# A list scheduler for TensorE in four quarters, with a new table of places, in a kernel of attention and two gated MLPs

## The chip, the cores and the metric

The kernel runs on one core of one Trainium2 chip. The metric is device time in microseconds of one execution. Three runs of the kernel before took 618.84, 619.43 and 620.29 us; their median is 619.43 us.

## What is computed

Four batches of 448 positions and 12 heads of 64 columns go through an attention with normed queries and keys, then through a gated MLP, then through a second one. Inputs are float32 values; the weights come to the kernel in 64-bit words. Cut to what matters:

```python
q_n, k_n = rmsnorm(q, g_q), rmsnorm(k, g_k)            # (4, 12, 448, 64)
attn = softmax(scale * q_n @ k_n.T); x = attn @ v      # -> (4, 448, 768)
h = relu(x @ w_in)                                     # 768 -> 1024
x = (h * sigmoid(conv3(h))) @ w_out                    # 1024 -> 768
y = (sigmoid(causal_conv5(x)) * (x @ w_val)) @ w2_out  # 768 -> 768
```

## The kernel before

Nothing is issued where it is written. The code calls a recorder, `Plan`, in place of the engines. `at(t, fn)` gives each step of the work (an event) a nominal time t; the events are sorted by it and run once, and each engine call in them becomes an operation with its data dependences, its possible engines ("ways") and its event's time. `Plan.order()` then simulates the chip and puts all operations in one order, and `Plan.emit` issues them in that order. All instructions of the profile therefore carry the line of `emit`, L545, and are told apart by their tiles.

The order comes from a list scheduler. An operation's urgency (`first`) is made of its event's nominal time, the length of work behind it (`tail`) and its event's entry in the table `OFFSETS`, which moves the operations of that event earlier or later by that many us. `forward` keeps a clock for each engine; again and again it takes the engine that can start something first, and of the operations that can start by then the most urgent one. For TensorE an operation of another shape than the one before (up to 64 rows, up to 64 columns, or neither) has `SWITCH` added to its urgency, and 0.1 us to its cost. `backward` finds the latest times, `MIX` blends these into the urgencies, and the best of `PASSES` passes is kept. Operations of one engine stay in the order found; between engines semaphores hold them to their data.

In the old clock TensorE is one engine that does one matmul after the other. A matmul whose output starts at a partition above 0, or that has 64 rows of input in the upper half, is costed at 0.022 us, because it runs beside the one before it.

The work: a unit is 128 query positions of two heads (or the 64 left over, of two pairs of heads). Its scores are matmuls of 64 rows, one head in the upper half of the rows and one in the lower, three float16 products each (high and low parts) or, for the groups in `FLAT`, one in float32. VectorE multiplies by the root of q's norm and finds the row maxima (`smax`), ScalarE takes the exponential, a high and a low part are made (`phi`, `plo`), a DMA or TensorE transposes, and `av` multiplies by the values. There are 21 units to a batch, 84 in all. The two MLPs of a batch run beside the attention of the next one; their matmuls have 128 rows and 448 or 384 columns. Batch 3's MLPs have nothing beside them.

Norms: `sum_q` and `sum_k` square and sum; `FOLD_Q0` to `FOLD_Q3` say how many times the squares are first folded in half on GpSimd. `rroots` takes the inverse root by three steps: with `ROOT_POOL` of the batch 0, three VectorE instructions each, with 1, four that may go to VectorE or GpSimd. `LEAVE_IN` of a batch says whether the gated tile leaves PSUM for SBUF (its low part can then be made on GpSimd), `X_SBUF` the same for the attention's result.

Times of the parts are in constants: `S_TQ` the nominal time at which the first group's q is turned, `W_IN` to `W_2` of the weights, `L_...` and `PC_...` what is added to an operation's cost on one of its ways when an engine is chosen.

Of the kernel before, what the change touches and what calls it, by code (L numbers as in the profile page):

```python
# [176 lines left out]
class Plan:  # L177
# [12 lines left out]
    AHEAD = 39.506  # L190
    URGENT = 0.644
    TICK = 10.24 / 3
    ENTRY = 3060.0

    SWITCH = 2.538

    PASSES = 4
    MIX = 0.913

    KEEP = 0.002  # L200

    SLACK_T = 1.769
    SLACK_L = 0.399
    CUSH = 0.0
# [344 lines left out]
def kernel(  # L549
# [540 lines left out]
    def prep(b, r, t0, tq, dq, tk_, dk, ahead):  # L1090
# [91 lines left out]
        def gain_k(i):  # L1182
            if flat:
                return
# [735 lines left out]
```

## Time and profile before

| | |
|---|---|
| span of the profiled execution | 618.4 us |
| the profiled execution's own time | 620.15 us |
| median of three runs | 619.43 us |
| TensorE matmuls busy | 594.4 us, 4747 instructions |
| VectorE busy | 491.2 us, 1124 instructions |
| ScalarE busy | 412.0 us, 797 instructions |
| GpSimd busy | 276.7 us, 330 instructions |

PE is TensorE's matmul, PEld its weight loads, DVE VectorE, ACT ScalarE, POOL GpSimd, SP the queue that issues most DMAs. A busy time is the union of an engine's instructions; matmuls are pipelined, so the time from one start to the next is shorter than the length of one. Some matmul records can be missing from a trace, so counts of matmuls in a row may be low. A wait is the idle time of an engine just before an instruction, put down to the last thing that released it.

### The profile page before, as it was taken

The numbers are of one execution on the slowest core, as the hardware profiler recorded it, in microseconds if no ns is written. First come the engines' busy times: TensorE is split into PE (matmuls) and PEld (weight loads), VectorE is DVE, ScalarE is ACT, GpSimd is POOL, SyncE is SP. The second block draws the span as 40 slices with busy tenths as digits, with TensorE's granted clock in tenths as the row PEclk, the third lists the DMA queues.
The fourth block names the chain that finished last, engine by engine and source line by source line (L and its number), as shares of the span: only waits on it lengthen the run. The fifth ranks groups of instructions, "written<-read, shape, count | busy, mean of one in ns | idle before, by whom it ended". The sixth has DMA issues, their size and how long they took to land.

```text
span 618.4 us, 12831 instructions
## 1 busy us (share of the span) xinstructions
PE 594.4 (96%) x4747; PEld 346.3 (56%) x4747; DVE 491.2 (79%) x1124; ACT 412.0 (67%) x797; POOL 276.7 (45%) x330
## 2 busy tenths in 40 slices
PE   5999999998999999999999999999999999999997
PEld 2666776555666555455555556455555656555554
DVE  6899999999999987898789785699898543567820
ACT  4887988889869886896567645778766543352221
POOL 2243644456755879587365751733564210140000
PEclk9999999999999999999999999999999999999999
DMA  7866649686839498975898579865564658000002
GB/s 205 195 153 166 164 124 242 149 206 135 165 103 225 99 181 159 215 185 130 176 158 144 112 161 192 155 118 100 92 127 95 117 120 136 14 1 1 1 13 77
DMA packets 230805, 82.10 MB, mean 133 GB/s; under 512 B 216864, under 2 KB 226646, under 8 KB 230742
## 3 DMA queue, kind: packets, MB, share of 16 engines
q1 hardware_dynamic: 229541, 79.71, 60.5%
q10 hardware_dynamic: 1200, 1.57, 1.0%
q8 instruction: 37, 0.61, 0.4%
q14 instruction: 27, 0.21, 0.1%
HBM read 38.59 MB, written 5.51 MB: 71 GB/s over the span
## 4 chain that ended last, share of the span: by engine, by line
PE 52%; DVE 24%; ACT 9%; DMA 6%; POOL 4%; issue 4%; SPq 1%; ACTq 0%; DVEq 0%; POOLq 0%
PE ps L545 52%; DVE ps L545 6%; DVE act L545 5%; DVE scr L545 4%; DVE w L545 4%; ACT p L545 3%; DMA pt<-p 2%; DVE half L545 2%; DMA act<-in_moe_w_out_dram 1%; ACT act L545 1%; SPq L545 1%; DVE ssq L545 1%; POOL tq L545 1%; DVE p L545 1%; POOL tk L545 1%
## 5 line engine op out<-in xcount | busy, mean ns | idle before, releaser
L545 PE MATMUL ps<-act,wo 128*128 128x448 f16 x576 | 125.4, 353 | 1.5 <-ACT ka L545 0.8
L545 DVE TENSOR_SCALAR_CACHE_REDUCE ps<-ps,root 128x448 f32<-128x448 f32 x168 | 109.3, 686 | 20.2 <-PE ps L545 19.8
L545 PE MATMUL ps<-act,wi 128*128 128x448 f16 x576 | 118.4, 353 | 1.3 <-DVE scr L545 0.7
L545 ACT ACTIVATE p<-ps,mx 128x448 f32<-128x448 f32 x154 | 91.4, 632 | 19.2 <-POOL mx L545 7.8
L545 PE MATMUL ps<-vv,pt 128*128 128x65 f16 (+5 forms) x1440 | 103.4, 206 | 0.0
L545 PE MATMUL ps<-w,act 128*128 128x384 f16 (+1 forms) x576 | 93.3, 327 | 0.9 <-ACT w L545 0.9
L545 POOL TENSOR_TENSOR p<-p,p 128x896 f16<-128x896 f32 x32 | 61.4, 1921 | 68.4 <-ACT p L545 59.3
L545 PE MATMUL ps<-act,wv 128*128 128x448 f16 x432 | 91.9, 353 | 0.0
L545 PE MATMUL ps<-ka,qa 64*128 64x448 f16 (+3 forms) x512 | 86.5, 415 | 2.5 <-ACT ka L545 1.3
L545 PEld LDWEIGHTS <-wi 128*128 128x128 f16 x576 | 53.7, 98 | 53.9 <-issue 9.2
L545 PEld LDWEIGHTS <-wo 128*128 128x128 f16 x576 | 55.1, 100 | 48.7 <-issue 8.1
L545 PEld LDWEIGHTS <-pt 128*128 128x128 f16 (+1 forms) x1344 | 64.0, 101 | 26.7 <-issue 7.8
L545 ACT ACTIVATE act<-ps 128x448 f16<-128x448 f32 (+3 forms) x80 | 42.4, 534 | 45.6 <-PE ps L545 25.2
L545 PEld LDWEIGHTS <-act 128*128 128x128 f16 (+1 forms) x576 | 48.6, 101 | 31.1 <-issue 5.3
L545 DVE SCALAR_TENSOR_TENSOR act<-ps,cw,act 128x446 f32<-128x446 f32 (+2 forms) x96 | 63.7, 674 | 0.7
L545 PEld LDWEIGHTS <-wv 128*128 128x128 f16 x432 | 40.9, 98 | 37.1 <-issue 3.0
L545 ACT ACTIVATE p<-p 128x896 f16<-128x896 f32 x56 | 53.2, 951 | 3.0 <-DMA pt<-p 2.5
L545 DVE SCALAR_TENSOR_TENSOR w<-w 128x768 uint32<-128x768 uint32 (+1 forms) x56 | 46.6, 832 | 0.4 <-POOL w L545 0.4
L545 DVE SCALAR_TENSOR_TENSOR scr<-ps,cw,scr 128x447 f32<-128x447 f32 x64 | 41.6, 673 | 0.8 <-ACT scr L545 0.7
L545 DVE TENSOR_TENSOR p<-p,p 128x896 f16<-128x896 f32 x24 | 28.5, 1188 | 12.7 <-ACT p L545 12.0
L545 ACT ACTIVATE osb<-ps 128x384 f32<-128x384 f32 x28 | 13.6, 489 | 32.7 <-PE ps L545 28.4
L545 DVE SCALAR_TENSOR_TENSOR act<-ps,act 128x448 f16<-128x448 f32 x48 | 29.7, 618 | 7.0 <-ACT act L545 7.0
(134 smaller groups left out, 938.9 us busy)
## 6 DMA issues: line engine op xcount, KB each, us to landing
w<-in_moe_w_in_dram SPq DMA_DIRECT2D x8, 768.0 KB, 5.9
w<-in_moe_w_out_dram SPq DMA_DIRECT2D x8, 768.0 KB, 4.5
kin<-in_k_dram SPq DMA_DIRECT2D x24, 224.0 KB, 3.5
qin<-in_q_dram SPq DMA_DIRECT2D x36, 128.0 KB, 3.2
act<-in_moe_w_out_dram SPq DMA_DIRECT2D x12, 384.0 KB, 4.1
w<-in_moe_w_val_dram SPq DMA_DIRECT2D x12, 384.0 KB, 3.3
out_dram<-osb SPq DMA_DIRECT2D x19, 192.0 KB, 2.6
vst<-in_v_dram SPq DMA_DIRECT2D x16, 224.0 KB, 3.6
```

Source lines behind the costliest of these rows:

```text
L545: getattr(getattr(nc, e), method)(*a, **k)
```

## The change

Three things change.

First, the clock in `forward`. TensorE has four quarters, `parts`: rows below or above 64 by columns below or above 64. A matmul occupies the quarters that it uses until its end; the next one starts when its own quarters are free, and no sooner than `ISSUE` (0.022 us) after the one before. One that follows another TensorE operation by data is ready `ISSUE` after that one's start. Second halves now have their full cost.

Second, the table `OFFSETS` is another: 820 entries in place of 1411, and about forty constants have other values.

Third, new options in the program, all off in the new constants (`K_PE`: keys turned by TensorE with float16 parts; `HALVES`: the transposes of a unit in two DMAs), and six options set otherwise: `FOLD_Q1` 0 to 1, `LEAVE_3` 1 to 0, `XSB_3` 1 to 0, `ROOTP_0` 0 to 1, `ROOTP_2` and `ROOTP_3` 1 to 0. TensorE's matmuls are the same ones as before.

```diff
 OFFSETS = {
...
-    ENTRY = 3060.0
-
-    SWITCH = 2.538
+    ENTRY = 3060.0
+    ISSUE = 0.022
+
+    SWITCH = 2.173
...
-    MIX = 0.913
-
-    KEEP = 0.002
-
-    SLACK_T = 1.769
-    SLACK_L = 0.399
+    MIX = 0.915
+
+    KEEP = 0.053
+
+    SLACK_T = 1.906
+    SLACK_L = 0.332
...
-            if self.region(out)[0] or (a[1].shape[0] == 64 and self.region(a[2])[0]):
-                return 0.022, f * n * a[1].shape[0] / (256 if self.region(out)[0] else 128), 0
-            return 0.0024 + f * max(n, 128 if wide else 64) / 2400, f * n * a[1].shape[0] / 128, 0
+            half, cols = a[1].shape[0] <= 64, a[0].shape[0] <= 64
+            rows = (2 if self.region(a[2])[0] else 1) if half else 3
+            part = (rows << 2 if self.region(out)[0] else rows) if cols else rows | rows << 2
+            columns = f * n * a[1].shape[0] / (256 if self.region(out)[0] else 128)
+            return 0.0024 + f * max(n, 128 if wide else 64) / 2400, columns, part
...
+        def taken(part):
+            return max(x for j, x in enumerate(parts) if part >> j & 1)
...
+        parts = [0.0] * 4
 
         def begin(i, e):
             t = max(free[e], hold[e], ready[i])
+            if e == "tensor":
+                t = max(t, taken(ops[i][0][e][0][2]))
...
+                before = max(t, *parts)
+                for j in range(4):
+                    if data >> j & 1:
+                        parts[j] = t + busy
...
-            free[e] = t + busy
+            free[e] = t + (self.ISSUE if e == "tensor" else busy)
+            if e == "tensor":
+                busy = max(0.0, t + busy - before)
...
-                hop = 0.0 if method.startswith("dma") or e == "tensor" == next(iter(ops[u][0])) else self.HOP[e] + self.CUSH
-                ready[u] = max(ready[u], end + hop)
+                hop = 0.0 if method.startswith("dma") else self.HOP[e] + self.CUSH
+                inside = e == "tensor" == next(iter(ops[u][0]))
+                ready[u] = max(ready[u], t + self.ISSUE if inside else end + hop)
...
-    S_TQ = 2.948
+    S_TQ = 4.204
...
-    FOLD_Q1 = 0
+    FOLD_Q1 = 1
...
-    LEAVE_3 = 1
+    LEAVE_3 = 0
...
-    XSB_3 = 1
-    ROOTP_0 = 0
+    XSB_3 = 0
+    ROOTP_0 = 1
     ROOTP_1 = 0
-    ROOTP_2 = 1
-    ROOTP_3 = 1
+    ROOTP_2 = 0
+    ROOTP_3 = 0
```

## Rows read from the trace of the kernel before

**Rows 1.** The page, engines: busy us, share of the span, instructions.

```profile
PE 594.4 (96%) x4747; PEld 346.3 (56%) x4747; DVE 491.2 (79%) x1124; ACT 412.0 (67%) x797; POOL 276.7 (45%) x330
```

**Rows 2.** Table by stretches: length; busy us of PE, PEld, DVE, ACT, POOL; clock; DMA.

```profile
0.00:15.00 15.00, 7.85 (x26) 4.20 (x26) 9.73 (x47) 6.69 (x11) 4.01 (x28) 1.00 0.80 207
15.00:55.00 40.00, 38.26 (x268) 27.31 (x269) 35.61 (x98) 34.95 (x72) 14.60 (x10) 1.00 0.75 181
55.00:95.00 40.00, 38.20 (x327) 27.77 (x326) 38.51 (x105) 33.90 (x67) 19.22 (x24) 1.00 0.52 149
95.00:138.00 43.00, 41.55 (x325) 23.80 (x326) 41.94 (x92) 36.04 (x67) 19.89 (x15) 1.00 0.80 193
138.00:191.00 53.00, 50.76 (x334) 31.10 (x332) 51.65 (x110) 44.61 (x90) 33.03 (x35) 1.00 0.63 143
191.00:400.00 209.00, 203.87 (x1800) 113.14 (x1801) 173.29 (x381) 150.25 (x292) 135.19 (x174) 1.00 0.82 163
400.00:525.00 125.00, 123.96 (x1163) 70.93 (x1161) 93.28 (x218) 78.19 (x151) 41.55 (x38) 1.00 0.61 113
525.00:600.00 75.00, 75.00 (x404) 39.24 (x402) 47.16 (x81) 24.44 (x46) 9.20 (x9) 1.00 0.02 4
600.00:618.40 18.40, 14.98 (x109) 8.78 (x107) 0.00 (x0) 2.94 (x6) 0.00 (x0) 1.00 0.22 74
```

**Rows 3.** Chain of waits: start us, us, what; 138 to 192 us, and the end.

```profile
184.08 1.35 DVE ps L545 x4
...
523.96 91.04 PE ps L545 x532
```

**Rows 4.** TensorE's waits from 15 to 600: total us, times, longest us.

```profile
PE ps L545 <- ACT p L545: 2.7, 6, 0.9
PE ps L545 <- DMA pt<-p: 2.7, 3, 1.0
PE ps L545 <- ACT act L545: 1.6, 4, 0.6
...
PE ps L545 <- issue: 0.2, 1, 0.2
```

**Rows 5.** Timeline of TensorE at 524 and 296: start us, us, what, count.

```profile
524.69 10.57 PE L545 MATMUL ps<-act,wi 128*128 128x448 f16 x55
...
296.16 0.32 PE L545 MATMUL ps<-w,act 128*128 128x384 f16 x1
296.42 1.31 PE L545 MATMUL ps<-ka,qa 64*128 64x448 f16 x12
297.66 0.24 PE L545 MATMUL ps<-vv,pt 128*128 128x64 f16 x2
```

**Rows 6.** Instruction groups (first 15 to 191, then whole span): busy us, mean ns, idle before.

```profile
L545 DVE TENSOR_SCALAR_CACHE_REDUCE ps<-ps,root 128x448 f32<-128x448 f32 x67 | 43.6, 685 | 4.0 <-PE ps L545 4.0
...
L545 DVE TENSOR_REDUCE ssq<-tq 128x14 f32<-128x896 f32 x6 | 6.4, 1062 | 0.0
...
L545 POOL TENSOR_TENSOR act<-scr,act 128x448 f16<-128x448 f32 x16 | 16.7, 1048 | 18.2 <-ACT act L545 14.9 <-DVE act L545 3.1
...
L545 DVE TENSOR_TENSOR act<-ps,act 128x448 f16<-128x448 f32 x16 | 9.7, 613 | 0.4 <-ACT act L545 0.4
```

**Rows 7.** Timeline of TensorE, float32 scores early and later.

```profile
11.31 3.20 PE L545 MATMUL ps<-ka,qa 64*128 64x448 f32 x8 [0.72 <-ACT ka L545]
14.44 0.51 PE L545 MATMUL ps<-ident,act 112*128 112x112 f32 x3
...
43.62 1.77 PE L545 MATMUL ps<-ka,qa 64*128 64x448 f32 x8 [0.61 <-ACT ka L545]
45.33 0.24 PE L545 MATMUL ps<-ident,act 24*128 24x24 f32 x1
```

**Rows 8.** The root's scratch tile: VectorE 15 to 62; durations ns min/median/max on GpSimd.

```profile
15.00:62.00 47.00, 5.32 (x20) 1.00 0.69 171
...
L545 POOL TENSOR_SCALAR half<-half x11: 222/223/1092, 216.4 to 456.5; 128x30 f32<-128x30 f32 x11
```

More of the change, by code (lines that the diff above doesn't have):

```diff
@@ L539, in forward @@
                     enter(u)
-        return result, max(free.values()), ends
+        return result, max(*free.values(), *parts), ends
     def emit(self, nc):
@@ L698 @@
     EARLY_W = 20
-    S_TQ = 2.948
-    S_DQ = 0.06
+    S_TQ = 4.204
+    S_DQ = 0.005
     S_K0 = 1.209
     S_K1 = 10.195
-    S_DK = 0.153
+    S_DK = 0.207
     S_LQ = 5.919
@@ L709 @@
     DT_2 = 6.044
-    DT_3 = 5.846
+    DT_3 = 5.855
     LAG = 2
@@ L713 @@
     C_GATE = 1.818
-    C_MUL = 2.115
+    C_MUL = 1.881
     C_HI = 2.538
-    C_LO = 3.349
+    C_LO = 3.529
     V_HI = 0.217
@@ L726 @@
     M_1 = -6.504
-    M_2 = -4.505
+    M_2 = -5.284
     M_3 = 4.463
-    D_IN = 2.169
+    D_IN = 2.515
     APART = 2.77
@@ L754 @@
     QD_ = 1.286
-    W_IN = -79.472
+    W_IN = -73.121
     W_IN_STEP = 0.252
@@ L758 @@
     W_OUT_STEP = 1.141
-    W_VAL = 21.2
+    W_VAL = 21.552
     W_VAL_STEP = 0.724
@@ L771 @@
     OUT_3 = 4
+    KPE0_1 = 0
+    KPE0_2 = 0
+    KPE1_0 = 0
+    KPE1_1 = 0
+    KPE1_2 = 0
+    KPE2_0 = 0
+    KPE2_1 = 0
+    KPE2_2 = 0
+    KPE3_0 = 0
+    KPE3_1 = 0
+    KPE3_2 = 0
+    HALF_0 = 0
+    HALF_1 = 0
+    HALF_2 = 0
+    HALF_3 = 0
     WIDE_0 = 1
@@ L789 @@
     L_ROOT = 0.045
-    L_QHI = -0.43
+    L_QHI = 0.252
     L_QLO = -0.306
@@ L793 @@
     L_NORM = 3.224
-    L_KHI = 1.704
-    L_KLO = 0.731
-    L_GLO = 1.042
+    L_KHI = 1.991
+    L_KLO = 0.724
+    L_GLO = 2.877
     L_MUL = 0.171
     L_MXA = 0.2
-    L_RS = 0.452
+    L_RS = 0.419
     MUL = 0.0
@@ L819 @@
     PC_M = 9.047
-    PC_X = 8.979
-    PC_G = 9.0
+    PC_X = 9.243
+    PC_G = 9.307
     PC_F = 8.843
-    PC_S = 0.3
+    PC_S = 0.265
     L_WF = 1.0
@@ L828 @@
     L_VHI = 1.568
-    L_VLO = 1.414
+    L_VLO = 1.035
     L_PHI = 2.172
-    L_PT = 4.537
+    L_PT = 4.191
     L_XHI = -0.121
-    L_GHI = 0.283
+    L_GHI = 0.44
     WIDE = [(0, r) for r, w in enumerate((WIDE_0, WIDE_1, WIDE_2)) if w]
@@ L842 @@
     FK = (FOLD_K0, FOLD_K1, FOLD_K2, FOLD_K3)
+    HALVES = (HALF_0, HALF_1, HALF_2, HALF_3)
     X_SBUF = (0, XSB_1, XSB_2, XSB_3)
@@ L845 @@
     FLAT = [(0, 0)] + [x for x, f in (((0, 1), FLAT0_1), ((0, 2), FLAT0_2), ((1, 0), FLAT1_0), ((1, 1), FLAT1_1)) if f]
+    K_PE = [((0, 1), KPE0_1), ((0, 2), KPE0_2), ((1, 0), KPE1_0), ((1, 1), KPE1_1), ((1, 2), KPE1_2), ((2, 0), KPE2_0), ((2, 1), KPE2_1), ((2, 2), KPE2_2), ((3, 0), KPE3_0), ((3, 1), KPE3_1), ((3, 2), KPE3_2)]
+    K_PE = [x for x, f in K_PE if f]
     events = []
@@ L1099, in prep @@
         flat = (b, r) in FLAT
+        k_pe = flat or (b, r) in K_PE
         g = b * NPR // 2 + r
@@ L1182, in gain_k @@
         def gain_k(i):
-            if flat:
+            if k_pe:
                 return
@@ L1191, in norm_k @@
             holds["tk", i if b == 0 or NTK == 2 else 0] = b, j
-            if flat:
+            if k_pe:
                 by = rr[:KR, cols(i)].rearrange("p (h c) -> p h c", h=2).unsqueeze(3).to_broadcast([KR, 2, KC, D])
@@ L1202, in low_k @@
             assert holds["kin", i] == holds["tk", i if b == 0 or NTK == 2 else 0] == (b, j)
-            if not flat:
+            if not k_pe:
                 sub(lean(L_KLO, S_LK), lo, x, hi)
@@ L1209, in turn_k @@
             holds["ka", (b * NPR + j) % NKA] = b, j
-            if flat:
+            if k_pe:
                 x = o.rearrange("p a c d -> p (a c d)").bitcast(F32).rearrange("p (c d) -> p c d", c=KC)
@@ L1214, in turn_k @@
                     nc.tensor.transpose(ps[:, c * KR : (c + 1) * KR], x[:, c], ident[:KR, :KR])
+                if not flat:
+                    to = ka[(b * NPR + j) % NKA]
+                    times(L_PT, to[:, 0], ps[:, 0:S], gcol)
+                    fma(to[:, 1], ps[:, 0:S], gcol, to[:, 0], ALU.subtract)
+                    return
                 times(L_PT, ka[(b * NPR + j) % NKA].rearrange("p a t -> p (a t)").bitcast(F32), ps[:, 0:S], gcol)
@@ L1359, in ptr @@
         u.t = pt[u.n % u.bufs]
+        if HALVES[u.b]:
+            for a in range(2):
+                turned(out=u.t[:, a * NB : (a + 1) * NB], in_=u.o[:, a].rearrange("p h t -> p (h t)"))
+            return
         turned(out=u.t, in_=u.o.rearrange("p a h t -> p (a h t)"))
```

233 rows, old and new, of the table OFFSETS are left out of this document.

## The prediction

> **What bounds the kernel now.** I read the engines' totals first. TensorE's matmuls are busy 594.4 of 618.4 us, 96%; VectorE has 79% and ScalarE 67% [rows 1]. So about 24 us of span hold no matmul, and everything else lies under matmuls. The profiled execution took 620.15 us, 1.75 more than its span; the sum below is made against it. It stands 0.7 above the 619.43 of the runs shown and inside their spread.
>
> Then the table by stretches [rows 2] says where the 24 us are: 7.15 in the first 15 us (loads and the first norms), 1.74 from 15 to 55, 1.80 to 95, 1.45 to 138, 2.24 to 191, 5.13 to 400, 1.04 to 525, none from 525 to 600, and 3.42 at the end, where the last result is evacuated and stored. The reader is to see a second thing in it: from 55 to 191 VectorE has 38.51 of 40, 41.94 of 43 and 51.65 of 53 us, as full as TensorE. The chain of waits agrees: in that part it goes from one VectorE piece to the next, and from 523.96 it is one run of 532 matmuls, 91.04 us long [rows 3]. What is won before 523 us therefore shifts the rest as a block and reaches the end whole.
>
> Third, what TensorE waited for between 15 and 600 us [rows 4]: ten releasers, of which the first three and the last stand in the rows, 12.6 us together, none above 2.7. Some 9.7 of them are on pieces of ScalarE, VectorE or GpSimd, at most 0.9 us at a time, 2.7 on the DMA that transposes the probabilities. These waits are short and spread; they are the kind that an order of instructions makes or unmakes. The order is what this change rewrites.
>
> Last, the matmuls themselves. In the last stretch 55 full-array matmuls of 448 columns take 10.57 us, with 0.35 for the last one's own length 0.189 each [rows 5]. Twelve matmuls of 64 rows, two score units in one block, take from 296.42 to 297.66, 1.24 us: six times 0.189 plus about 0.1. So the two halves of a pair run at once, and the second costs nothing. The matmul of 384 columns before them (0.162 by its columns) has the next one 0.26 behind it: a block of 64-row work costs some 0.1 us at its entry and 0.1 at its exit. I counted 93 blocks of half-array work in the timeline, the first at 11.31 us [rows 5, 7]: 93 x 0.2 = 18.6 us that no idle column shows.
>
> **The change, part by part.**
>
> *The clock in quarters.* The old clock charges 22 ns for every second half; the chip charges nothing. That overcharge is, in the plan: 48 float16 score units x 3 pairs x 22 ns = 3.2 us, 8 remainder score units x 3 x 66 = 1.6, their 8 value products x 21 x 22 = 3.7, four remainder output tiles x 18 x 22 = 1.6, float32 units about 1.4: 11.5 us over the program. On the chip TensorE reaches its next operand earlier than the plan thinks, and that is where short waits come from. The new clock leaves at most one 22 ns issue per block, 2 us. It removes no matmul. What it can remove is bounded by the 12.6 us of waits [rows 4] below and by none above; a new order can also make as many new ones. I take a third, 4.2 us: the waits on other engines' pieces (9.7) are the ones that better times touch, the DMA's 2.7 and the order's own trade-offs stay. What is late next is VectorE, which between 55 and 191 has only 3.9 us left over its three windows [rows 2].
>
> *Blocks of half-array work.* With quarters, a pair's successor in the same quarter may start 22 ns before any full-array matmul, so a ready pair goes first whatever its urgency, and units merge more often; the extra for a change of shape falls from 2.538 to 2.173, which pulls the other way. I take 5 blocks fewer, 5 x 0.2 = 1.0 us; bounds 15 fewer (-3.0) and 7 more (+1.4).
>
> The Trainium skill, in "TensorEngine Tiling (Array Packing)", section Key Properties, says that a change of tiling mode drains the engine while different tiles run at the same time. By its rule the unit merged away is the gain and not the second half; the 0.1 us at entry and exit [rows 5] agree with it.
>
> *Work moved off VectorE early.* The root of batch 0 may go to GpSimd step by step: two groups that aren't first, of eleven VectorE instructions each, nine of them in the three steps. From 15 to 62 us VectorE spends 5.32 us on 20 of these 22 [rows 8], 0.27 each, so the steps are 18 x 0.27 = 4.8 us. The squares of q in batch 1 are folded once on GpSimd, so three sums of 896 elements, 1.06 us each, become half as long (-1.6) against three additions on GpSimd. GpSimd is 36 to 62% busy there [rows 2]. On TensorE this is worth nothing beyond the third above, since it idles only 1.74 us from 15 to 55. Bounds: -2 and, if GpSimd's slower root is late, +1.
>
> *Work moved back onto VectorE late.* Batch 3 keeps its gated tile and its x in PSUM: eight subtractions leave GpSimd (1.05 us) for VectorE (0.61) [rows 6], and six on tiles of 384 instead of 448 columns likewise, 8 x 0.61 + 6 x 0.53 = 8.1 us of VectorE. The eight belong to the last stage, where VectorE has 47 of 75 us [rows 2]; the six come with batch 3's values, mostly before 525, where it has 93 of 125. The roots of batches 2 and 3 lose their choice of GpSimd and three instructions in twelve. Cover: TensorE from 400 on waits 1.04 us in all, so nothing is gained and nothing lost. If the cover goes, a PSUM bank is held 0.6 us longer; bound +1.
>
> *The start.* The first group's q is turned 1.26 us later by its nominal time. The first score pairs take 0.78 us each, four from 11.31 to 14.44; four later ones, from 43.62 to 45.33, take 1.71 us with the 0.2 of their block, 0.38 each [rows 7]: at the start TensorE runs at half rate, the lower (1.2 GHz) of its two levels, though the granted clock of that window reads 1.00. Where the change to the higher one falls is a matter of phase. I take 0. Bounds: -1.6, half of those 3.13 us, and +1.6.
>
> *The end.* Evacuation and store, 3.42 us, unchanged: 0.
>
> Sum: -4.2 - 1.0 = -5.2. Span 618.4 - 5.2 = 613.2, the execution 1.75 more, 614.95, and the runs' median 0.7 below the profiled one, 614.3. I say 614.5.
>
> **The rivals.**
>
> *A, no change.* The waits don't come from the clock's error but from what no clock knows: when a semaphore arrives, how long a transpose lands. For it: ten releasers, none dominant [rows 4]. Against: most are compute pieces, and these have steady lengths, as the row maxima at 685 ns in the mean of 67 [rows 6]. Then as many waits return, at 619.4, give or take 1.2.
>
> *B, slower.* The rule that a ready pair goes before a full-array matmul displaces the matmuls that feed VectorE. A block of one unit is 0.57 + 0.2 = 0.77 us, and where VectorE has no queue it stands idle for it. From 15 to 191 us there are 67 row maxima, 33 units [rows 6], and from 55 us on VectorE has 4% left or less [rows 2]. If every third block hits, that is 11 x 0.77 = 8.5 us later, less some 4 of the forecast's gain: +4.5, 624. It decides from seven hits on (5.4 us, the whole gain). For it: the full VectorE. Against: VectorE's own waits for TensorE in that time are 4.0 us before row maxima [rows 6], so its queue is mostly filled.
>
> *C, GpSimd blocked.* A root step on GpSimd has a median of 0.22 us and a maximum of 1.09 [rows 8]. If all twelve steps of a group were that long, 13.1 us against VectorE's 9 x 0.27 = 2.4, 10.7 late; the nominal lead of k is 3.236 units of 2.39 us, 7.7, so 3.0 late for each of two groups, +6.0 on the forecast: 620.5. The Trainium skill, "SBUF — State Buffer", section Who interferes with whom, gives the reason: a VectorE instruction with two SBUF inputs and a GpSimd one that reads SBUF exclude each other for a whole instruction. The maximum agrees with it, the median says that it is rare.
>
> **How the numbers follow.** Changes under 0.2% (1.24 us) can't be told from none here. Forecast 0.56, its own range 608.5 to 618; A 0.15; B 0.24; C 0.05. The low end is two thirds of the waits and ten blocks (-8.4 - 2.0, 609), a little below for the start; the high end is B, 623.5. Faster: the forecast and a quarter of A, 0.59. Same: the rest of A's middle, half of C and the edges of the others, 0.15. Slower: B, the rest of C and A's upper edge, 0.26.
>
> **What would show it.** TensorE's waits from 15 to 600 at 8 to 9 us instead of 12.6, its busy time down by about 1 through fewer blocks, VectorE below 95% between 55 and 95. The last stretch of pure matmuls keeps its 91 us and starts about 5 earlier. Wrong: waits of 12 or more (A), VectorE idle behind TensorE between 55 and 191 (B), TensorE or ScalarE waiting for the root (C), or TensorE's busy time up by 2 or more, which means more blocks.

## The result, and the profile after

The changed kernel takes 614.02 us (median of 20 runs, 612.15 to 620.60); the kernel before took 620.84 in 20 runs beside it (618.84 to 624.19). The ratio is 0.9901, with a 95% interval of 0.9883 to 0.9919: about 1% faster. The profiled execution took 614.43 us with a span of 612.6, so 5.8 less span than before.

The runs of the changed kernel differ by TensorE's granted clock, which has to be known to read what follows: the five runs with a clock of 1.000 over the whole program have a median of 612.94 us, the run with the lowest, 0.988, took 620.60. Of the kernel before most runs have 0.999 or 1.000, 48 of the 66 that stand beside the experiments below.

The engines' totals of the changed kernel (busy us, share of the span, instructions), the answer to [rows 1]:

```profile
PE 588.7 (96%) x4747; PEld 344.4 (56%) x4747; DVE 483.8 (79%) x1145; ACT 413.8 (68%) x796; POOL 270.8 (44%) x301
```

The same 4747 matmuls keep TensorE busy for 5.7 us less than in [rows 1]: that is as much as the span lost. Idle time hardly changed, 23.9 us against 24.0. The table by stretches, with the columns of [rows 2], says where it lies:

```profile
0.00:15.00 15.00, 7.72 (x25) 4.33 (x26) 9.70 (x47) 6.70 (x11) 4.30 (x28) 1.00 0.81 209
15.00:55.00 40.00, 37.69 (x274) 28.32 (x274) 36.69 (x91) 33.23 (x66) 15.25 (x21) 0.96 0.70 160
55.00:95.00 40.00, 36.68 (x340) 28.62 (x338) 37.16 (x100) 36.65 (x71) 22.95 (x38) 1.00 0.57 158
95.00:138.00 43.00, 42.38 (x349) 24.57 (x348) 38.23 (x80) 40.20 (x77) 30.81 (x25) 1.00 0.85 195
138.00:191.00 53.00, 51.06 (x348) 31.45 (x346) 52.26 (x124) 44.29 (x88) 30.27 (x36) 1.00 0.66 153
191.00:400.00 209.00, 203.99 (x1796) 112.15 (x1796) 168.88 (x404) 148.70 (x289) 127.71 (x126) 1.00 0.82 164
400.00:525.00 125.00, 124.99 (x1151) 69.89 (x1150) 93.65 (x224) 74.40 (x142) 39.49 (x32) 1.00 0.62 110
525.00:600.00 75.00, 75.00 (x408) 39.76 (x407) 47.22 (x82) 27.66 (x53) 0.00 (x0) 1.00 0.03 9
600.00:612.60 12.60, 9.17 (x74) 5.30 (x71) 0.00 (x0) 1.97 (x4) 0.00 (x0) 1.00 0.24 79
```

From 15 to 95 us TensorE is idle for 5.63 us (2.31 and 3.32), where it was 3.54 before; from 95 to 525 it is idle for less than before in each window, and from 400 to 600 it never stops. Waits were moved to an earlier place, not removed; the DMA that transposes the probabilities is nearly gone from them (0.4 after 2.7), and others took its place. From 15 to 55 the granted clock is 0.96, a number that [rows 2] doesn't have anywhere.

TensorE's waits from 15 to 595 us (total us, times, longest us), the answer to [rows 4]. There are eight releasers, and together they make 12.8 us; ten made 12.6 before:

```profile
PE ps L500 <- DVE scr L500: 3.7, 5, 1.8
PE ps L500 <- ACT p L500: 2.8, 4, 1.3
PE ps L500 <- ACT pt L500: 2.8, 4, 1.2
...
PE ps L500 <- DMA pt<-p: 0.4, 1, 0.4
```

The longest single wait is 1.8 us, against 1.0 before [rows 4]. The chain of waits from 408.90 us to 609.18 is TensorE alone; its second half:

```profile
508.12 101.07 PE ps L500 x661
```

**Where the 5.7 us of matmul time were.** The next table counts only the matmuls of the scores (the tile `ka`): window, its length, busy us and records of PE, clock. First the kernel before, then the changed one:

```profile
0.00:55.00 55.00, 16.79 (x47) 1.00 0.76 188
55.00:138.00 83.00, 21.79 (x98) 1.00 0.67 171
...
sum 525.00, PE 86.55; mean PE 17.31
```

```profile
0.00:55.00 55.00, 15.08 (x46) 0.97 0.73 174
55.00:138.00 83.00, 17.35 (x100) 1.00 0.72 177
...
191.00:400.00 209.00, 26.24 (x210) 1.00 0.82 164
400.00:525.00 125.00, 12.88 (x120) 1.00 0.62 110
sum 525.00, PE 81.13; mean PE 16.23
```

The scores became 5.42 us shorter, and they are the same scores. The timeline of TensorE shows how. In the kernel before, one head of a float32 score unit, then other work, then a head alone again (start us, us, what, count; the time of a block is read from its start to the start of the row behind it):

```profile
28.81 1.02 PE L545 MATMUL ps<-ka,qa 64*128 64x448 f32 x2
29.76 1.09 PE L545 MATMUL ps<-ident,p 128*128 128x128 f32 x8
30.78 1.02 PE L545 MATMUL ps<-ka,qa 64*128 64x448 f32 x2
31.73 0.55 PE L545 MATMUL ps<-ident,p 128*128 128x128 f32 x3
```

In the changed kernel both heads stand in one block:

```profile
31.85 1.02 PE L500 MATMUL ps<-ka,qa 64*128 64x448 f32 x4
32.80 0.55 PE L500 MATMUL ps<-ident,act 128*128 128x128 f32 x2
```

One head alone takes 0.95 us (28.81 to 29.76, 30.78 to 31.73), both together take 0.95 (31.85 to 32.80). In float16 it is the same: a lone head (kernel before) and a pair (changed kernel) take 0.67 each:

```profile
273.40 0.74 PE L545 MATMUL ps<-ka,qa 64*128 64x448 f16 x3
274.07 0.30 PE L545 MATMUL ps<-vv,pt 128*128 128x64 f16 x4
```

```profile
272.79 0.74 PE L500 MATMUL ps<-ka,qa 64*128 64x448 f16 x6
273.46 0.34 PE L500 MATMUL ps<-vm,pt 128*128 128x130 f16 x3
```

So the second half of a pair costs nothing only where it runs beside the first. The timeline of before has 12 lone float32 heads, that of after 5; a pair is 0.95 together and 1.90 apart, so this is (12 - 5) / 2 x 0.95 = 3.3 us. In float16 it is 8 blocks of a lone head against 7, 0.3 us. The rest isn't divided here. Part of it is the entry and exit of blocks of half-array work: there are 15 changes of shape fewer, 173 after 188, which is 7 or 8 blocks. At the prediction's 0.2 us for a block that is an estimate of 1.5 us, and some of it is in the 3.3 already, since a pair that is rejoined is also a block less.

**Which part of the change joined them.** The old clock charged 0.022 us for a second half wherever it stood, so nothing kept the two heads together. That this is the reason is argued, not shown. In the order as issued, 116 of the 168 pairs of score products have another TensorE operation between their heads in the kernel before, and 32 in the changed one; but that count misleads. Of the 116, 94 have only other score products of the same block there, and such a block costs no more: six float16 products issued as first, first, second, second, first, second head take 0.68 us (329.36 to 330.04, kernel before), issued as first, second, second, first, second, first 0.67 (the block at 272.79). Pairs that other work splits are 22 in the kernel before and 23 in the changed one. What fell is the dear kind: 6 of the 22 are float32, and 3 of the 23 (one of their six lone heads stands in a block with a pair, so that the timeline shows five).

Nor are two heads in one block always as cheap as a pair. Of these two blocks of the changed kernel, of four float32 heads each, the first is issued as first, second, second, first head and takes 1.70 us (97.14 to 98.84), the other as first, first, second, second, and takes 2.69 (100.37 to 103.06):

```profile
97.14 1.77 PE L500 MATMUL ps<-ka,qa 64*128 64x448 f32 x8
...
100.37 2.76 PE L500 MATMUL ps<-ka,qa 64*128 64x448 f32 x8
```

In e2 the second one is issued as first, second, first, second and takes 2.22 us (104.97 to 107.19). So the order is a part of it; what the rest waits for is not shown.

**The clock that is lost early.** The timeline of the changed kernel at 41 us, with the waits in brackets:

```profile
41.07 1.77 PE L500 MATMUL ps<-ka,qa 64*128 64x448 f32 x8
43.99 0.24 PE L500 MATMUL ps<-ident,act 24*128 24x24 f32 x1 [1.15 <-DVE scr L500]
...
45.32 1.30 PE L500 MATMUL ps<-ident,p 128*128 128x128 f32 x7 [0.83 <-ACT p L500]
46.55 2.28 PE L500 MATMUL ps<-ka,qa 64*128 64x448 f32 x4
48.76 2.02 PE L500 MATMUL ps<-ident,act 128*128 128x128 f32 x11
50.61 0.40 PE L500 MATMUL ps<-vm,pt 128*128 128x130 f32 x2
```

After two waits of 1.15 and 0.83 us, a group of four score matmuls takes 2.21 us (46.55 to 48.76), where the same four take 1.37 in e12 below (46.63 to 48.00). The window from 46 to 50 has a granted clock of 0.59, so most of it is at 1.2 GHz, the lower of the two levels:

```profile
46.00:50.00 4.00, 4.00 (x14) 2.49 (x15) 3.89 (x13) 3.33 (x7) 1.47 (x2) 0.59 0.12 23
```

Those four microseconds count as busy time; part of the gain is given back there without an idle column showing it. The clock of 0.997 over the profiled span says how much: 0.003 x 612.6 = 1.8 us.

### The profile page after: what moved, and what is told of

It is laid out like the page before. It is cut to its first block, busy times and chain, and to the rows that moved or that the text cites. A ratio compares the mean times of both kernels' runs of the same rounds, so it can differ in the third digit from the quotient of the medians.

```text
span 612.6 us, 12783 instructions
## 1 busy us (share of the span) xinstructions
PE 588.7 (96%) x4747; PEld 344.4 (56%) x4747; DVE 483.8 (79%) x1145; ACT 413.8 (68%) x796; POOL 270.8 (44%) x301
## 4 chain that ended last, share of the span: by engine, by line
PE 70%; DVE 14%; ACT 5%; DMA 4%; issue 3%; POOL 2%; SPq 1%; DVEq 0%; ACTq 0%; POOLq 0%
PE ps L500 70%; DVE act L500 3%; DVE w L500 3%; DVE ps L500 3%; DMA act<-in_moe_w_out_dram 2%; DVE scr L500 2%; ACT act L500 1%; DVE half L500 1%; DVE ssq L500 1%; ACT p L500 1%; DMA w<-in_moe_w_out_dram 1%; DMA ka<-tk 1%; SPq L500 1%; DVE root L500 1%; ACT w L500 1%
## 5 line engine op out<-in xcount | busy, mean ns | idle before, releaser
L500 PE MATMUL ps<-act,wo 128*128 128x448 f16 x576 | 123.1, 353 | 1.1 <-DVE act L500 1.1
L500 POOL TENSOR_TENSOR p<-p,p 128x896 f16<-128x896 f32 x40 | 76.5, 1915 | 65.5 <-ACT p L500 51.7
L500 PE MATMUL ps<-act,wv 128*128 128x448 f16 x432 | 90.3, 353 | 0.3 <-DVE act L500 0.3
L500 PE MATMUL ps<-w,act 128*128 128x384 f16 (+1 forms) x576 | 88.5, 326 | 0.4 <-ACT osb L500 0.4
L500 PE MATMUL ps<-ka,qa 64*128 64x448 f16 (+3 forms) x512 | 81.1, 418 | 0.8 <-ACT ka L500 0.7
L500 PE MATMUL ps<-vv,pt 128*128 128x65 f16 (+5 forms) x1440 | 80.0, 205 | 0.2 <-ACT pt L500 0.2
L500 ACT ACTIVATE act<-ps 128x448 f16<-128x448 f32 (+4 forms) x89 | 46.8, 532 | 42.1 <-DVE ps L500 21.9
L500 PEld LDWEIGHTS <-act 128*128 128x128 f16 (+1 forms) x576 | 48.5, 101 | 33.4 <-issue 5.0
L500 DVE SCALAR_TENSOR_TENSOR act<-ps,cw,act 128x446 f32<-128x446 f32 (+3 forms) x96 | 62.0, 674 | 0.3
L500 PEld LDWEIGHTS <-pt 128*128 128x128 f16 (+1 forms) x1344 | 51.4, 101 | 17.5 <-issue 6.4
L500 ACT ACTIVATE ps<-ps 128x448 f32<-128x448 f32 x32 | 16.5, 538 | 25.3 <-PE ps L500 25.3
```

What stands on the lines that cost most here:

```text
L500: getattr(getattr(nc, e), method)(*a, **k)
```

## The experiments

The theories were these. **P**: the heads of a pair now stand together, and this is the gain. **W**: the gain lies in waits, which the places and the order of the table set. **O**: the six options move work between engines, and this is the gain. Later **H**: waits of a microsecond or two early in the program are followed by a stretch at 1.2 GHz, and this sets how much of the gain is left. In e1, e2, e3 and e10 to e12 the finished order is edited, so that nothing else is planned anew; in e4 to e8 the scheduler plans again. Ratios are to the kernel before in the same session. It took 620.84 us beside the result, and on three chips 621.93 beside e1 to e4, 622.23 beside e5 to e8 and 622.02 beside e9 to e12. So times of two sessions are compared by their ratios. A pair is called split here where other work than score products stands between its heads.

**e1: the kernel before, its heads rejoined**

```diff
+    def paired(self, seq):
...
+            if all(at[d] < at[lo] or d == lo for d in self.ops[hi][1]):
+                seq.insert(at[lo] + 1, seq.pop(at[hi]))
+            elif all(at[u] > at[hi] for u in users[lo]):
+                seq.insert(at[hi] - 1, seq.pop(at[lo]))
...
-        for i, e in self.order():
+        for i, e in self.paired(self.order()):
```

> The order of before, and in it nothing but this: of the 168 products of 64 rows whose two heads could run at once, 116 have another TensorE operation between the heads; 55 moves bring a second head up to its first one (51) or a first head down to its second (4), wherever the data allow, and 22 pairs stay apart. Clock, table and options are those of before. Theory P (the gain is TensorE time: heads that were issued apart ran one after the other): a float16 product saves 0.19 us, a float32 one 0.75, a lone block its 0.2, so 4 to 6 us faster than before, with TensorE's busy time down by as much. Rival W (the gain is in how the order meets the other engines, as the prediction had it): the waits take it back, within 1 us of before or slower, since the places no longer fit.

Measured: 621.76 us against 621.93, ratio 0.9994 (0.9976 to 1.0012). No gain. The scores' matmuls fell from 86.55 to 84.34 us and TensorE's busy time from 594.4 to 593.0, but its waits from 15 to 600 rose from 12.6 to 13.3, and the span is 618.3 after 618.4. The 55 moves brought 94 pairs together; 22 stayed apart, and the float32 ones of the first 55 us are among them: there the scores take 16.70 us, as before (16.79). Of the 94 pairs, 90 had only score products of their own block between their heads, and only four were split, two of them float32. By the lone blocks above these four are worth 2 x 0.95 + 2 x 0.19 = 2.3 us, about what the scores lost; the 90 gave nothing. So P's 4 to 6 us could not come here, since the dear pairs were not joined. The waits took back half of what TensorE won, as W has it; but what was left, 0.7 us, is less than the interval can tell.

**e2: the changed kernel, 8 more pairs joined**

The same `paired` on the changed kernel's order.

> The order of after with the same moves: 32 of 168 pairs are apart there, 8 moves can be made, 22 stay. P: 1 to 2 us faster than after. W: the same as after within 0.5 us, or slower.

Measured: 618.74 us, ratio 0.9945 (0.9916 to 0.9974), clock 0.992 in the profile. No gain over the changed kernel (0.9901 in the result, 0.9936 in e9) can be seen. It was no test of P: all but one of the pairs that the 8 moves joined had only score products between their heads, and 22 of the 23 split pairs stayed.

**e3: the changed kernel, 17 late float16 units taken apart**

The three second heads of a unit (`x`) are issued behind the next full-array matmul (`mark`); the first heads stay.

```diff
+    def apart(self, seq, most):
...
+            k = last + 1
+            for y in x:
+                seq.remove(y)
+            k = seq.index(mark) + 1
+            seq[k:k] = x
...
-        for i, e in self.order():
+        for i, e in self.apart(self.order(), 24):
```

> The order of after, with the three second-head products of 17 float16 units moved behind the next full-array matmul, in the second half of the program. P: each unit pays 0.57 us for its second head and 0.2 for another block, 17 x 0.77 = 13 us slower than after, a little less where TensorE waited anyway: 9 to 13. W: hidden in part by waits, under 4 us slower.

Measured: 625.01 us, ratio 1.0067 (1.0039 to 1.0095): slower than the kernel before, and by the ratios (1.0067 against 0.9901) some 10 us over the changed one. One run of the eight took 635.99 us; the median of the others is 624.87. TensorE's busy time is 599.5, 10.8 more. In two of the 17 units the heads stood apart already, so this is 0.72 for each of the other 15; the lone block of the timeline is 0.67. The scores in the two late windows of this kernel, against 26.24 and 12.88 above:

```profile
191.00:400.00 209.00, 30.34 (x210) 1.00 0.81 161
400.00:525.00 125.00, 19.66 (x120) 1.00 0.59 104
```

This is the plainest result. Where TensorE doesn't wait, a pair apart costs the whole of its second half, and about all of it reaches the end. The waits stayed the same (12.4 us).

**e4: only the clock changed (old table, old constants, old options)**

```diff
+    ISSUE = 0.022
...
+            half, cols = a[1].shape[0] <= 64, a[0].shape[0] <= 64
...
+                t = max(t, taken(ops[i][0][e][0][2]))
...
+            free[e] = t + (self.ISSUE if e == "tensor" else busy)
```

> The new clock (quarters) with before's table, constants and options; its order has 55 pairs apart instead of 116. P: half of the gain and more comes with the clock, 2 to 5 us faster than before, less what a table costs that was made for another clock. W: slower than before by 2 us or more, because the table's places belong to the old clock.

Measured: 636.11 us, ratio 1.0227 (1.0203 to 1.0250). P's expectation was missed, W's side was right. Its order has 55 of the 168 pairs apart, after 116, but 30 of them are split by other work, after 22, and 8 of these are float32, after 6. So the new clock by itself doesn't rejoin the dear pairs. Span less TensorE's busy time is 33.4 us, after 24.0, and the granted clock is 0.981; that this comes of places which belong to the old plan is likely and not shown.

**e5: only the table and the constants changed (old clock)**

The changed kernel with the old `forward`: the lines of e4 the other way round.

> The old clock with after's table, constants and options; its order has 118 pairs apart and 214 changes of shape, before has 116 and 188. P: no faster than before; 26 more changes at 0.1 us and places that don't fit, 2 to 8 us slower. Rival T (the table and the options carry the gain): 2 us faster than before or more.

Measured: 647.84 us, ratio 1.0379 (1.0305 to 1.0453); clock 0.967. 118 pairs are apart, as many as in the kernel before, and 32 of them are split, 4 in float32. So neither the clock alone (e4) nor the table alone has fewer split pairs than the kernel before, and only both together bring the float32 ones down to 3.

**e6 and e7: the options alone, and everything but the options**

```diff
-    FOLD_Q1 = 0
+    FOLD_Q1 = 1
-    LEAVE_3 = 1
+    LEAVE_3 = 0
-    XSB_3 = 1
+    XSB_3 = 0
-    ROOTP_0 = 0
+    ROOTP_0 = 1
-    ROOTP_2 = 1
-    ROOTP_3 = 1
+    ROOTP_2 = 0
+    ROOTP_3 = 0
```

e6 is the kernel before with these lines, e7 the changed kernel with them the other way round.

> Before with the six options set as in after, planned anew by the old clock: 125 pairs apart, 209 changes of shape. P: slower than before by 1 to 5 us (21 more changes are 2.1 us, 9 more pairs apart 1.7 or more). Rival O (work moved off VectorE between 15 and 165 us is the gain): 2 to 4 us faster than before.

> After with the six options set back as in before, planned anew by the new clock: 46 pairs apart and 200 changes of shape, after has 32 and 173. P: 27 changes are 2.7 us, 14 pairs 2.6 or more, so 4 to 8 us slower than after. O: slower too, by 2 to 4, but with VectorE busier between 55 and 138 and TensorE's busy time the same.

Measured: e6 644.48 us, ratio 1.0296 (1.0200 to 1.0393), 125 pairs apart, 32 of them split, 12 in float32; e7 632.44 us, 1.0131 (1.0073 to 1.0189), 46 apart, 36 of them split, 4 in float32. The options make nothing faster with the old table, so O fails there. Each of the two has a plan and a clock of its own (0.976 and 0.986 in the profiles), so what e7 lost tells what the old options cost in that plan, and not what they are worth on the chip.

**e8: the changed kernel, one constant nudged**

```diff
-    KEEP = 0.053
+    KEEP = 0.054
```

> After with KEEP at 0.054 instead of 0.053, a change that means nothing on the chip, planned anew: 32 pairs apart, 179 changes of shape. It measures what planning anew alone costs, for e4 to e7. If the table's places are a fit to one plan: 1 to 4 us slower than after. If they are not: the same within 1 us.

Measured: 619.67 us, ratio 0.9949 (0.9914 to 0.9985). The changed kernel has 0.9901 (0.9883 to 0.9919) in the result and 0.9936 (0.9912 to 0.9960) in e9, so what this nudge costs is between nothing and some 3 us, and the runs can't tell it from nothing. The split pairs are the same 23. The theory of a fit to one plan, which foresaw 1 to 4 us, is left open; planning anew by itself is not shown to cost what e4 to e7 lost against the changed kernel, 12 us and more by the ratios. Still e4 to e7 can't divide the gain between clock, table and options: each is slower than both kernels, by more than the whole gain.

**e9: the changed kernel again, unedited, on the chip of e10 to e12**

> The changed kernel itself again, on the chip and beside the runs of the three others of this set, so that they are compared with it and not with before alone. It should be about 1% faster than before; where its profile has a stretch at the lower clock near 46 us, its time should be longer by one to two us than where it has none.

Measured: 618.19 us, ratio 0.9936 (0.9912 to 0.9960), clock 0.991 to 0.996 in all seven runs. In its profile the two waits of 1.15 and 0.83 us are there, and the clock is not lost behind them:

```profile
44.71 0.24 PE L500 MATMUL ps<-ident,act 24*128 24x24 f32 x1 [1.15 <-DVE scr L500]
...
46.03 1.29 PE L500 MATMUL ps<-ident,p 128*128 128x128 f32 x7 [0.83 <-ACT p L500]
```

```profile
46.00:50.00 4.00, 3.87 (x24) 2.69 (x25) 4.00 (x14) 4.00 (x9) 0.76 (x1) 1.00 0.02 4
```

The 15 matmuls behind them take 2.58 us (47.26 to 49.84), after 4.06 in the profile above (46.55 to 50.61). e3, whose order is the same up to there, has both waits too (1.14 and 0.83), and reads 1.00. So the waits alone don't bring the clock down. The lost clock lies elsewhere here (rows of the timeline from 67 us, and the window around them):

```profile
67.07 0.49 PE L500 MATMUL ps<-vm,pt 128*128 128x130 f32 x2 [1.50 <-ACT pt L500]
...
71.95 2.42 PE L500 MATMUL ps<-ka,qa 64*128 64x448 f16 x12
```

```profile
65.00:80.00 15.00, 12.66 (x74) 9.10 (x72) 9.73 (x26) 10.90 (x21) 9.51 (x17) 0.66 0.62 141
```

Twelve score matmuls take 2.36 us (71.95 to 74.31), after 1.24 in [rows 5]. The wait of 1.50 us ahead of it is longer than any of the kernel before. That the time would be one to two us shorter without a stretch near 46 us, as was expected, did not come: the clock was lost at another place.

**e10: the changed kernel, 7 early float32 units taken apart**

As e3, for float32 units in the order in which they stand, the second head behind the next full-array matmul.

> After, with the second head's float32 product of seven early units (batches 0 and 1) moved behind the next full-array matmul. P: 0.75 us for the head that ran beside the other, 0.2 for another block, 7 x 0.95 = 6.6 us slower than after, as in the second half of the program. Rival V (early on VectorE is the bound, TensorE's own time is hidden): 0 to 2 us slower, with TensorE's busy time up by 6 and its waits down by 4 or more.

Measured: 621.84 us, ratio 0.9986 (0.9959 to 1.0014). Three of its twelve runs took over 630 us; the median of the other nine is 621.53, 3.3 over e9. Seven second heads of 0.95 us would be 6.7, and V allowed 2. So early, too, a split pair costs time, though not the whole: part of it fills waits, which are 10.2 us from 15 to 600 in the profile, after 12.8 in the changed kernel's and 14.4 in e9's. Splitting seven gives back most of the 3.8 us that the change won on this chip. The clock has a part in it that can't be taken out. Runs that read 1.000 took 617.07, 617.17 and 630.41. In the profiled one, of 625.33 us, TensorE is at the lower level from 46 to 65 us, behind a wait of 1.15 us that ends at 44.68, without a gap in its work (window, its length, then as in [rows 2]):

```profile
46.00:65.00 19.00, 19.00 (x72) 12.86 (x71) 10.23 (x30) 9.04 (x19) 7.31 (x16) 0.50 0.24 49
```

**e11: the changed kernel, the 23 root steps of batch 0 back on VectorE**

```diff
+            if e == "gpsimd" and "vector" in self.ops[i][0]:
+                to = self.ops[i][0][e][2][0]
+                if tuple(to.shape) == (128, 30) and to.name.startswith(("half", "root")):
+                    e = "vector"
```

> After in its own order, only that the 23 steps of batch 0's inverse roots that GpSimd takes between 32 and 59 us are issued on VectorE, at the same places: some 23 x 0.19 = 4.4 us more on VectorE in a stretch where it has 9.3 of 10 us. O (the moved root is part of the gain): 2 to 4 us slower than after. P: within 1 us of after.

Measured: 615.47 us, ratio 0.9909 (0.9877 to 0.9942). It isn't slower than e9's 618.19, so the root on GpSimd is no part of the gain as measured; O fails here as well. Its clock is better: four of eight runs have 0.999 or more, none of e9's seven. And it lacks the wait of 1.15 us ahead of the transposes; where there were 1.15 and 0.83, one short wait is left:

```profile
45.10 1.30 PE L513 MATMUL ps<-ident,p 128*128 128x128 f32 x7 [0.32 <-ACT p L513]
```

It has other waits instead, of 1.08 us before 38.50 and of 1.69 before 73.69, and the clock reads 1.00 behind both. So no length of a wait decides by itself. Whether it is slower than the changed kernel at an equal clock is open: its runs at 0.999 or more begin at 614.6, but in another session.

**e12: the changed kernel, one wait filled**

The float32 scores of the unit at 41 us are computed twice, into the same place, so that TensorE works where it waited for 1.15 us.

```diff
+        k = max(at[x], at[y]) + 1
+        return seq[:k] + [(x, "tensor"), (y, "tensor")] * times + seq[k:]
...
-        for i, e in self.order():
+        for i, e in self.filled(self.order(), 7, 1):
```

> After, with the two float32 score products of one unit issued a second time, 0.75 us of TensorE work just before its wait of 1.15 us at 42.84 (the output is the same, and VectorE comes to it later anyway). Theory H (the two waits before 46.7 us are why the granted clock falls to half there): no stretch at the lower clock near 46 us, and 1 to 2 us faster than after. Without H: the same time within 0.5 us, or 0.7 slower, and the stretch is still there.

Measured: 615.27 us, ratio 0.9902 (0.9879 to 0.9925), with more work. One run of the twelve took 623.30; the median of the others is 615.13, 3.1 below e9. Eight of the twelve have a clock of 0.999 or more, none of e9's seven. Its timeline:

```profile
41.15 2.53 PE L544 MATMUL ps<-ka,qa 64*128 64x448 f32 x12
44.08 0.24 PE L544 MATMUL ps<-ident,act 24*128 24x24 f32 x1 [0.40 <-DVE scr L544]
...
45.40 1.29 PE L544 MATMUL ps<-ident,p 128*128 128x128 f32 x7 [0.83 <-ACT p L544]
46.63 1.44 PE L544 MATMUL ps<-ka,qa 64*128 64x448 f32 x4
48.00 1.37 PE L544 MATMUL ps<-ident,act 128*128 128x128 f32 x11
49.20 0.40 PE L544 MATMUL ps<-vm,pt 128*128 128x130 f32 x2
```

The wait of 1.15 became 0.40, and the same 15 matmuls behind it take 2.57 us (46.63 to 49.20) where they took 4.06 (46.55 to 50.61). This timeline alone is no proof of H: e9 and e3 keep the clock at this place without the filler. For H speak the twelve runs, which keep their clock more often with the filler than e9's seven do without. That the wait of 1.15 us is what brings the clock down is likely and not shown: at 65 to 80 us, where e9 lost it, e12's profile reads 1.00 as well.

## Why the prediction was right, and where its reason was wrong

The time was right: 614.5 forecast, 614.02 measured. The mechanism that carried four fifths of the forecast was not what happened, so that the number fits is luck for that part.

**The step that failed** is "It removes no matmul. What it can remove is bounded by the 12.6 us of waits", and with it the term of -4.2 for the waits. They went from 12.6 to 12.8. I said that "waits of 12 or more" would show A, no change; the waits are there, and the kernel is faster all the same, since the gain lies in TensorE's own time, which I had bounded at the blocks. No matmul went, but second heads that had run by themselves no longer do. The premise behind it, "the two halves of a pair run at once, and the second costs nothing", was read from one block of [rows 5] where they stand together, and taken for all. I reckoned that the old clock charges too much by 22 ns a half; it charged too little, by some 0.9 us for a lone float32 head and 0.6 for a float16 unit's three. Rows that show it were in the trace of before: the four above at 28.81 to 31.73. The premise needed a count of how often they stand together, and I made none. The 22 ns of the old clock may be why the pairs were split, but no run shows it: what the runs show is what a split pair costs (e3), and that the changed kernel has three split float32 pairs fewer.

The Trainium skill, "TensorE: Matmul & The Clock Gate", section "Why this matters for your kernels", says that one matmul with few rows takes as long as a full one, and that only several at once gain. The lone head at 0.947 us beside the pair at 0.954 agrees. I had used a page on what a pair saves and not asked when it is a pair.

**Blocks of half-array work**: -1.0 forecast from 5 blocks fewer. There are 7 or 8 fewer, 1.5 us at the same price. Right in kind, too small; the price itself was not measured apart.

**Early work off VectorE**: 0 on TensorE, and so it seems. VectorE is 93% busy from 55 to 95 (37.16 of 40), below the 95% that I had named. In e11 the root went back to VectorE without a loss.

**Late work back on VectorE**: 0, right. From 525 to 600 TensorE is busy for 75.00 of 75 us, GpSimd went from 9.20 us to none.

**Start and end**: 0 and 0, right. The end keeps 3.43 us without a matmul, and the first scores still start at 11.35 and run at half rate, as the prediction read them, though the granted clock reads 1.00 there:

```profile
11.35 3.36 PE L500 MATMUL ps<-ka,qa 64*128 64x448 f32 x8 [0.72 <-ACT ka L500]
```

Where the change to the higher level falls is not fixed even for one program: the three transposes behind these scores still take 0.82 us here (from 14.64), and 0.51 in e9 (from 14.69).

**The rivals.** B, that a ready pair starves VectorE, did not come: its wait for TensorE before row maxima from 15 to 191 us is 4.9 us, after 4.0. C, the root late on GpSimd, did not come either. Six of its 23 steps in the changed kernel, of one kind (ns min/median/max):

```profile
L500 POOL TENSOR_TENSOR half<-root x6: 236/237/944, 32.2 to 57.5; 128x30 f32<-128x30 f32 x6
```

Long ones exist, 0.94 us against a median of 0.24, but nothing waits for the steps; no releaser of TensorE's is the root.

**What no part of the prediction had** is the clock. At 1.000 the changed kernel is at 612.94, 7.9 below the 620.84 of before; 1.1 of it (614.02 less 612.94) is given back in the median there, and more in e9, where 618.19 is 3.8 below its 622.02. The forecast of 614.5 stands between these, by luck in part.

**What stays open.** That a pair apart costs its second half is shown (e3, in part e10), and so is that the changed kernel has fewer lone float32 heads and 5.42 us less of scores. That joining them is enough is not: e1 joined only two of the six float32 pairs, and its 0.7 us were too few to see. Which part of the change joined them is open too: of the six split float32 pairs the new table alone leaves four (e5), the new clock alone makes them eight (e4), and both lost more than the gain. Nor do the runs tell why one profile loses the clock at 46 us, another at 69 and a third nowhere, behind the same waits.

## What to carry to other kernels

Before a cost model is corrected, count where its case holds: a matmul that is free beside its partner is as dear as the partner when it is alone, and a plan that books it as free has no reason to keep it there. Look for lone halves in the timeline first: they count as busy time, and no wait shows them. Count them by what stands between the two: other products of the same block cost nothing in most of these blocks, other work cost the whole half. And here a table of places and the clock that it came with did not stand apart (e4, e5), so to see what one part is worth, edit the finished order.

## What the runs showed of the hardware

A float32 score head of 64 rows takes 0.95 us alone and 0.95 with the other head beside it; in float16 it is 0.67 and 0.67.

TensorE fell to 1.2 GHz in the midst of a program in which it is 96% busy, after waits of 1.15 and 0.83 us (46 to 50 us) and, in e9, after one of 1.50 (69 to 79 us). The same two waits left the clock at 1.00 in e3 and e9, and waits of 1.08 and 1.69 us did in e11. Over the 20 runs of the changed kernel a granted clock lower by 0.01 goes with 5.5 us more; 0.01 of the span is 6.1. The Trainium skill, "TensorE: Matmul & The Clock Gate", section "Part 1: The HAM clock gate (the "warmup" mystery)", says that activity lifts the clock from its lower level. e12 is in line with that, where eight of twelve runs kept their clock with work in place of a wait, and none of e9's seven without it; e10 is not plainly so, where TensorE was busy without a gap from 46 to 65 us and stayed at a granted clock of 0.50. A stretch at the lower level cost 1.5 us here (15 matmuls in 4.06 us after 2.57), and filler work was worth more than it cost.
